# Transfers and weight steps of a fused attention and expert kernel, put at other places of its order

## The chip, the cores and the metric

The kernel runs on one core of a Trainium2 chip. The metric is device time in microseconds, from the start of the program to its end. Three runs of the kernel before took 948.88 to 951.73 us, 950.14 in the median; 0.3% of that is 2.9 us.

## What is computed

Two stages, the second on the output of the first. Attention has 4 batches, 8 heads, 576 positions and 64 values a head; the scores get a causal mask and a bias from a running sum of `s`:

```
scores = q @ k.T / sqrt(64) + minimum(-(cum[i] - cum[j]), 0), causal, cum = cumsum(max(s, 0))
x = (softmax(scores) @ v), heads side by side: 2304 tokens x 512
p = domain_probs / sum(domain_probs)
out = sum over 4 experts e of p[:, e] * (relu(x @ w1[e]) @ w2[e])      # w1: 512 x 1024, w2: 1024 x 512
```

All is float32. The kernel splits each matmul operand into a high part and a rest and adds three products.

## The kernel before

**Three phases.** In the first, attention is planned by a small scheduler (class `Sched`), and expert 0 is computed on seven groups of token tiles (`GROUPS0`, numbered 0 to 6, two or three tiles of 128 tokens each) as soon as their tokens are there, whole for groups 0 to 4 and with the second half of its hidden columns alone for groups 5 and 6. Group results that are ready during attention go to DRAM (`o_d`, "spilled": groups 0 to 2), since their place in SBUF is not free yet. The second phase is what is left of this list (`prog`): the second layer of group 3 and all of groups 4, 5 and 6. The third phase takes the other expert halves (`HALVES`, seven pairs of an expert and half its hidden columns). In it 768 tokens at a time (`PAIRS`, three of them, called g = 0, 1, 2) pass through a first and a second layer, each with seven block products instead of eight, as in Strassen's scheme. The work list has 6 x 3 items and a last one alone (`LONE`: the first half of expert 0, only for g = 2). The order is first layer of item 0, first layer of item 1, second layer of item 0, first layer of item 2, and so on, so that the second layer of the last item stands alone at the end.

**Products.** Each product (`product`) is 12 matmuls on 384 columns. The first layer multiplies in the order 1, 6, 5, 7, 2, 4, 3, the second layer in the order 1, 6, 2, 5, 7, 3, 4. In the second layer the bank of product 1 is copied by ACT (`pass_on`) before product 6 goes on adding to it. Behind each product, `after(o)` runs steps that a table names: operands of the next second layer ("1" to "7": ACT writes the high part, DVE or POOL the rest; "s3" and the like: a sum by DVE that an operand needs) and one step from the list `side`, which holds the splits of the next expert's weights (`w_steps`: sums of weight blocks, then per block ACT the high part and DVE or POOL the rest). `ALL` is the table for the second layer of the last item but one. The last second layer had no steps.

**Sums of operands.** Products 5, 7, 6 and 3 of the first layer read sums of token blocks. `sums_of(g)` makes them in the second phase: it fetches four blocks of g (for g = 1 and 2 from `xf_d` into one of 6 temporary buffers; for g = 0 both parts from `x_d` into operand buffers, which POOL then joins), and POOL makes four sums, each of an add and a split in two instructions. Each sum is stored to `xs_d` (768 KB). For g = 0 the sums also stay in SBUF (`held`), as first operands of the third phase. Operand buffers are a ring of 7 (768 KB each).

**What sets the order.** Each engine works through its instructions in the order in which they were written, and all transfers are issued by one queue, SP. In the second phase the steps (fetches, sums, stores, weight loads and weight splits) carry a position in microseconds of planned PE time, `spent`, which each matmul raises by its planned duration (0.1735 for 384 columns, 0.12 for 256). A step is written when `spent` reaches its position; steps beyond the end follow at the end. So a position says where an instruction stands in every queue and not when it runs. Between the steps stand the loads that belong to `prog` itself: a group's input (`load_x`, into the one buffer `xg`) right behind the last first-layer product of the group before, and the gates of a token block (`prob0`, into one of two buffers `osb`) at the first eviction that needs them. The evictions of the second phase (DVE, `evict0`) multiply a bank by the gates into `acc`. Behind all that stood the 20 loads that bring the spilled results back into `acc`, and then the gates of the first item of the third phase.

The lines that rows name: L1077 fetches blocks for the sums, L1094 stores a sum, L1050 and L1057 fetch operands, L930 a group's input, L1031 gates, L1123 and L1128 weights, L1267 returns spilled results; L1061 adds and subtracts, L448 makes a rest, L461 and L463 a high part; L946 is the rest of a hidden half, L1203 the eviction of the second phase, L1282 the matmuls of the third, L1290 `pass_on`, L1293 the gating, L1405 the updates of `acc`.

Positions before: the sums of g = 1 from 10, those of g = 2 from 28, those of g = 0 from 47; in each, the fetches come first, then the sums 4.7 apart, and each sum's store stands where the next sum begins:

```
yield now, lambda o=o, d=d, a_=a_, b_=b_, op=op: split(o, d, a_, b_, op)
now += 4.7
yield now, lambda o=o: store(o)
```

Of the kernel before, what the change touches and what calls it, by code (L numbers as in the profile page):

```python
# [36 lines left out]
T_PREP = (10.0, 28.0, 47.0)  # L37
T_LOAD = 6.0
T_W1 = 44.0
T_W2 = 53.0  # L40
# [3 lines left out]
ALL = {4: "4", 1: "1", 2: "2", 6: "6", 5: "5", 7: "7", 3: "s3 3"}  # L44
# [286 lines left out]
def body(ctx, tc, qk, qkv0, vp, s, dp, w1, w1s, w2, w2s, out):  # L331
# [731 lines left out]
    def sums_of(g, held):  # L1063
# [7 lines left out]
        def load(part):  # L1071
            if held is not None and not held:
                held.update({o: x_tile() for o in PRODUCTS})
# [21 lines left out]

        for at, part in zip((-8.0, -4.0, 0.0, 4.0) if held is not None else (0.0, 2.0, T_LOAD, T_LOAD + 2.0), order):
            yield at, lambda part=part: load((part,))
        now = 8.0
# [4 lines left out]
        for o, d, a_, b_, op in ((5, (1, 1), (1, 0), (1, 1), ALU.add), (7, (1, 0), (0, 0), (1, 0), ALU.subtract),  # L1103
                                 (6, (0, 0), (1, 1), (0, 0), ALU.subtract), (3, (0, 1), (0, 1), (0, 0), ALU.subtract)):
            yield now, lambda o=o, d=d, a_=a_, b_=b_, op=op: split(o, d, a_, b_, op)
            now += 4.7
            yield now, lambda o=o: store(o)
# [23 lines left out]
    def w_steps(which, begin=False, lone=False):  # L1131
# [24 lines left out]
        def split(o, e):  # L1156
# [8 lines left out]
            if o == (6 if neg else 2) and not begin:  # L1165
# [4 lines left out]
                 ((1, "DVE"), (2, "POOL"), (5, "DVE"), (6, "DVE"), (7, "POOL"), (3, "DVE"), (4, "POOL")) if lone else  # L1170
# [21 lines left out]

    def prob0(b_):
# [6 lines left out]
    def evict0(gi, dt, t):  # L1200
        n0, n1 = GROUPS0[gi][0] * P, GROUPS0[gi][-1] * P + P
        for b_, u0, u1 in blocks_of(n0, n1):
# [5 lines left out]
    steps = sorted(((T_PREP[n] + t, n, k, f) for n, g in enumerate((1, 2, 0)) for k, (t, f) in enumerate(sums_of(g, None if g else held))),  # L1208
                   key=lambda x: x[:3])
    steps.append((T_PREP[1] + 1.0, 9, 0, lambda: (stage_w1(*HALVES[0]), stage_w2(*HALVES[0]))))  # L1210
# [6 lines left out]
    steps.append((T_W1 - 4.0, 9, 0, lambda: w_begin(1, w1_first)))  # L1217
# [7 lines left out]
    for i, x in enumerate(prog):  # L1225
# [16 lines left out]
        else:  # L1242
# [4 lines left out]
            else:  # L1247
                if x[3].done is None:
                    nc.sync.dma_start(out=o_d[dt * P:(dt + 1) * P, n0:n1], in_=tok["osb", x[1]][:, 0:n1 - n0])
                spilled.append((dt, n0, n1))  # L1250
# [14 lines left out]
    for dt, n0, n1 in spilled:  # L1265
        for b_, u0, u1 in blocks_of(n0, n1):
            nc.sync.dma_start(out=acc[dt][b_][:, u0 - TG * b_:u1 - TG * b_], in_=o_d[dt * P:(dt + 1) * P, u0:u1])  # L1267
# [184 lines left out]
    for w_i, (n, g) in enumerate(work):  # L1452
# [20 lines left out]
        if g == 2 and more:  # L1473
            w2_next = w_steps(2, lone=n + 1 == LONE)
            k = 8 if n + 1 == LONE else 4
            side.extend(w2_next[:k])
            del w2_next[:k]
        second_layer(w_i, n, g, plan(steps, EARLY if w_i + 2 < len(work) else ALL if w_i + 2 == len(work) else {}))
# [34 lines left out]
```

## Time and profile before

| | |
|---|---|
| median of three runs | 950.14 us |
| profiled execution | 948.41 us, span 946.6 us |
| PE busy | 915.2 us (97%) |
| DVE, ACT, POOL busy | 706.9, 491.7, 518.2 us |
| transfers | 201.34 MB, mean 213 GB/s |

The profile is of one execution; its times start with the span. PE is TensorE's matmuls, DVE VectorE, ACT ScalarE, POOL GpSimd, SP the queue that issues transfers (SPq in rows). A busy PE is not PE at its peak. A row of a timeline merges like instructions that follow each other, and says in brackets how long the engine was idle before them and what ended that. The granted clock is 1.00 when TensorE runs at full speed and falls towards 0.5 when the throttle halves it.

### The profile page before, as it was taken

What the parts mean: (1) busy time and instruction counts of PE and PEld (TensorE: products, weight loads), DVE (VectorE), ACT (ScalarE), POOL (GpSimd) and SP (SyncE); (2) the same over time, 40 slices, a digit from 0 to 9 for tenths busy, and PEclk for the clock granted to TensorE, in tenths of its full rate; (3) what the DMA queues carried; (4) which work ended last, traced back from release to release, by engine and by line L of the source; (5) the groups of instructions that cost most, each with busy time, mean ns of one, the idle gap of its engine ahead of it and who ended that gap; (6) DMA issues with size and microseconds to landing.
All of it is one profiled execution on the core that took longest, in us unless ns stands there. A gap on an engine that the chain in (4) does not pass through costs nothing.

```text
span 946.6 us, 16511 instructions
## 1 busy us (share of the span) xinstructions
PE 915.2 (97%) x5566; PEld 885.1 (94%) x5566; DVE 706.9 (75%) x1599; ACT 491.7 (52%) x1117; POOL 518.2 (55%) x540
## 2 busy tenths in 40 slices
PE   9999999999999977799999999999999999999996
PEld 6889999999999967699999999999999999999996
DVE  7878887887842536487787878778877887787885
ACT  6898999998841202234443344353344533443542
POOL 4688787887726487016541644362456317443562
PEclk9999999999999997899999999999999999999999
DMA  6788888778426984897666587656875667864201
GB/s 170 189 251 246 224 230 225 224 226 244 133 95 193 337 285 151 283 376 256 220 205 220 196 294 241 202 174 225 292 250 172 214 220 234 287 214 156 84 1 66
DMA packets 132239, 201.34 MB, mean 213 GB/s; under 512 B 11496, under 2 KB 107820, under 8 KB 132156
## 3 DMA queue, kind: packets, MB, share of 16 engines
q1 hardware_dynamic: 132156, 200.30, 66.2%
q8 instruction: 44, 0.72, 0.3%
q14 instruction: 39, 0.32, 0.1%
HBM read 157.34 MB, written 29.05 MB: 197 GB/s over the span
## 4 chain that ended last, share of the span: by engine, by line
PE 54%; DVE 2%; DMA 2%; SPq 1%; ACT 1%; POOL 1%; issue 0%; ACTq 0%; DVEq 0%; POOLq 0%
PE pb L1282 46%; PE mo L1282 8%; DMA osb<-p_d 1%; DVE t L1293 1%; SPq L1267 1%; DMA acc<-o_d 1%; DVE acc L1405 0%; DVE hT_r L448 0%; DVE t L1322 0%; ACT hT_r L461 0%; DVE w1l L448 0%; POOL w1l L448 0%; ACT w1h L461 0%; POOL hT_r L448 0%; ACT pb L1290 0%
## 5 line engine op out<-in xcount | busy, mean ns | idle before, releaser
L1282 PE MATMUL pb<-x,w1h 128*128 128x384 f32 x1064 | 272.1, 336 | 7.0 <-DMA x<-x_d 7.0
L1282 PEld LDWEIGHTS pb<-x,w1h 128*128 128x128 f32 x1064 | 192.5, 189 | 9.2 <-ACT t L1315 8.8
L1282 PE MATMUL pb<-x,w1l 128*128 128x384 f32 x532 | 178.4, 335 | 0.0
L1290 ACT ACTIVATE pb<-pb 128x384 f32<-128x384 f32 x112 | 53.0, 474 | 204.2 <-DVE t L1322 112.1
L448 POOL TENSOR_TENSOR hT_r<-t,hT_r 128x768 fp32r<-128x768 f32 x18 | 33.8, 1876 | 176.3 <-PE pb L1282 147.8
L1282 PE MATMUL pb<-hT_r,w2h 128*128 128x384 f32 x432 | 109.6, 334 | 0.0
L1282 PEld LDWEIGHTS pb<-x,w1l 128*128 128x128 f32 x532 | 100.3, 189 | 0.0
L461 ACT ACTIVATE hT_r<-t 128x768 fp32r<-128x768 f32 x76 | 64.0, 843 | 55.6 <-PE pb L1282 44.3
L762 ACT ACTIVATE a<-a,mx 128x576 f32<-128x576 f32 (+4 forms) x136 | 81.0, 597 | 12.6 <-DVE mx L754 9.3
L1405 DVE TENSOR_TENSOR acc<-pb,acc 128x384 f32<-128x384 f32 x152 | 78.7, 549 | 11.8 <-ACT pb L1290 7.2
L940 PE MATMUL mo<-xg,w1h 128*128 128x384 f32 (+1 forms) x304 | 79.9, 332 | 3.1 <-DMA xg<-x_d 3.1
L1282 PEld LDWEIGHTS pb<-hT_r,w2h 128*128 128x128 f32 x432 | 78.0, 188 | 0.0
L448 DVE TENSOR_TENSOR hT_r<-t,hT_r 128x768 fp32r<-128x768 f32 x58 | 58.4, 1006 | 24.4 <-ACT hT_r L461 23.8
L456 POOL TENSOR_SCALAR a<-a,sm 128x576 f32<-128x576 f32 (+5 forms) x111 | 61.0, 556 | 28.4 <-DVE sm L770 14.4
L1282 PE MATMUL pb<-xg,w2h 128*128 128x384 f32 x288 | 73.3, 335 | 0.7 <-ACT pb L1290 0.7
L1282 PE MATMUL pb<-hT_r,w2l 128*128 128x384 f32 x216 | 72.2, 334 | 0.0
L1322 DVE TENSOR_TENSOR t<-pb,t 128x384 f32<-128x384 f32 x78 | 39.8, 552 | 40.4 <-ACT t L1315 27.5
L1061 DVE TENSOR_TENSOR t<-t 128x768 f32<-128x768 f32 (+1 forms) x42 | 64.6, 1544 | 0.1
L448 POOL TENSOR_TENSOR xg<-t,xg 128x768 fp32r<-128x768 f32 x19 | 43.0, 2261 | 31.8 <-PE pb L1282 31.8
L940 PEld LDWEIGHTS mo<-xg,w1h 128*128 128x128 f32 x304 | 52.7, 193 | 5.6 <-DMA xg<-x_d 4.2
L818 DVE TENSOR_TENSOR aTl<-T,aTh 128x256 fp32r<-128x256 f32 (+2 forms) x103 | 51.2, 508 | 4.9 <-ACT aTh L461 3.6
L1293 DVE SCALAR_TENSOR_TENSOR t<-t,osb 128x768 f32<-128x768 f32 x40 | 47.0, 1177 | 10.3 <-DMA osb<-p_d 9.0
(245 smaller groups left out, 2346.1 us busy)
## 6 DMA issues: line engine op xcount, KB each, us to landing
x<-xs_d SPq DMA_DIRECT2D x68, 768.0 KB
x<-x_d SPq DMA_DIRECT2D x55, 768.0 KB
xs_d<-x SPq DMA_DIRECT2D x12, 768.0 KB
osb<-p_d SPq DMA_DIRECT2D x19, 384.0 KB
w1r<-in_w1s_dram SPq DMA_DIRECT2D x7, 1024.0 KB
w2r<-in_w2s_dram SPq DMA_DIRECT2D x7, 1024.0 KB
KK<-AB_r SPq DMA_DIRECT2D x24, 288.0 KB
xg<-x_d SPq DMA_DIRECT2D x16, 384.0 KB
```

Of the source, the lines that this page charges most:

```text
L448: (nc.gpsimd if e == "POOL" else nc.vector).tensor_tensor(out=out, in0=in0, in1=in1, op=ALU.subtract)
L456: (nc.gpsimd if e == "POOL" else nc.vector).tensor_scalar(out, in_, scale, 1.0 if bias is None else bias, op0=ALU.mult, op1=ALU.mult if bi ...
L461: nc.scalar.activation(out, in_, AF.Copy)
L762: nc.scalar.activation(z[0:n, 0:bb], z[0:n, 0:bb], AF.Exp, bias=tok["mx", c][0:n, k:k + 1], scale=-1.0, accum_out=tok["sm", c][0:n])
L818: nc.vector.tensor_tensor(out=dst, in0=src, in1=h_.bitcast(F32), op=ALU.subtract)
L940: nc.tensor.matmul(t[:, 0:w], wl[q][:, dc, o:o + P], xgt[:, l, dc, 0:w], start=(u == 0), stop=(u == 3 * KD - 1))
L1061: (nc.gpsimd if e == "POOL" else nc.vector).tensor_tensor(out=out, in0=in0, in1=in1, op=op)
L1282: nc.tensor.matmul(ts[u], wv[wl][:, k, 128 * u:128 * u + 128], x[xl_][:, k, :], start=start and k == 0 and n == 0, stop=k == 1 and n == 2, ...
L1290: nc.scalar.activation(out[u], in_[u], AF.Copy)
L1293: (nc.gpsimd if e == "POOL" else nc.vector).scalar_tensor_tensor(out=out, in0=in0, scalar=0.0, in1=in1, op0=ALU.max, op1=op)
L1322: nc.vector.tensor_tensor(out=tmp[name][:, u], in0=ts[u], in1=tmp[name][:, u], op=ALU.add)
L1405: nc.vector.tensor_tensor(out=d, in0=ts[u], in1=d, op=ALU.add)
```

## The change

Seven things move. (1) The positions of the sums stand in a table of their own, `SUM_AT`: fetches, the first sum, the first store. For g = 1 the fetches stand at 0.3 to 1.2, the sums from 2.0 and the stores from 13.5; for g = 2 at 6, 6.5, 16 and 18, from 23 and from 32; for g = 0 at 31 to 36, from 42 (four joins, then sums from 49.6) and from 57. Sums and stores follow each other 4.7 apart. (2) The seven operand buffers that stay in SBUF are asked for in another order. (3) The first weight halves are fetched at 20 and 25, one by one, instead of both at 29. (4) The first layer's weight sums begin at 36 instead of 40 and its splits at 42 instead of 44; the second layer's sums at 50 instead of 53. (5) The 20 return loads (`back`) stand at 48.0 instead of at the end. (6) In the last second layer, operand 3 is made behind product 1 and operand 4 behind product 6; before, both were made in the second layer before it. (7) The weight blocks of the last second layer are split in the order 5, 2, 6, 1, 7, 3, 4, with the sums and the first four inside the second layer before it and the other three inside the last one.

```diff
--- before.py
+++ after.py
@@ -34,14 +34,16 @@
 HALVES = [(e, s) for e in range(1, E) for s in range(2)] + [(0, 0)]
 LONE = len(HALVES) - 1
 LG = 2
-T_PREP = (10.0, 28.0, 47.0)
-T_LOAD = 6.0
-T_W1 = 44.0
-T_W2 = 53.0
+SUM_AT = {1: ((0.3, 0.6, 0.9, 1.2), 2.0, 13.5), 2: ((6.0, 6.5, 16.0, 18.0), 23.0, 32.0), 0: ((31.0, 31.5, 32.0, 36.0), 42.0, 57.0)}
+T_RAW = (20.0, 25.0)
+T_W1 = 42.0
+T_W2 = 50.0
+T_BACK = 48.0
 START = {7: "4"}
 EARLY = {1: "1", 6: "s5", 5: "s7", 7: "2", 3: "s6", 4: "4"}
 REST = {1: "6 5", 6: "s3 7", 5: "3"}
-ALL = {4: "4", 1: "1", 2: "2", 6: "6", 5: "5", 7: "7", 3: "s3 3"}
+ALL = {1: "1", 2: "2", 6: "6", 5: "5", 7: "7"}
+END = {1: "s3 3", 6: "4"}
 LAST = {4: "s5 s7", 3: "s6"}
 FIRST = {1: "s5 s7 1", 6: "s6 6", 5: "2 s3", 4: "5", 3: "7 3"}
 PRODUCTS = (1, 6, 5, 7, 2, 4, 3)
@@ -1070,7 +1072,7 @@
 
         def load(part):
             if held is not None and not held:
-                held.update({o: x_tile() for o in PRODUCTS})
+                held.update({o: x_tile() for o in (3, 4, 1, 2, 5, 7, 6)})
             for i, j in part:
                 if held is None:
                     raw[i, j] = temp()
@@ -1093,9 +1095,9 @@
         def store(o):
             nc.sync.dma_start(out=xsv[g, SUMS[o]], in_=flat4(blocks[o]))
 
-        for at, part in zip((-8.0, -4.0, 0.0, 4.0) if held is not None else (0.0, 2.0, T_LOAD, T_LOAD + 2.0), order):
+        loads, now, out_at = SUM_AT[g]
+        for at, part in zip(loads, order):
             yield at, lambda part=part: load((part,))
-        now = 8.0
         if held is not None:
             for i, j in order:
                 yield now, lambda i=i, j=j: join(i, j)
@@ -1103,8 +1105,9 @@
         for o, d, a_, b_, op in ((5, (1, 1), (1, 0), (1, 1), ALU.add), (7, (1, 0), (0, 0), (1, 0), ALU.subtract),
                                  (6, (0, 0), (1, 1), (0, 0), ALU.subtract), (3, (0, 1), (0, 1), (0, 0), ALU.subtract)):
             yield now, lambda o=o, d=d, a_=a_, b_=b_, op=op: split(o, d, a_, b_, op)
+            yield max(now, out_at), lambda o=o: store(o)
             now += 4.7
-            yield now, lambda o=o: store(o)
+            out_at += 4.7
 
     stage = {}
 
@@ -1167,7 +1170,7 @@
 
         order = (tuple((o, "DVE") for o in ((1, 2, 4, 3, 6, 5, 7) if which == 1 else (1, 2, 3, 4, 6, 5, 7))) if begin else
                  ((5, "POOL"), (1, "POOL"), (2, "POOL"), (6, "POOL"), (4, "POOL"), (7, "DVE"), (3, "DVE")) if which == 1 else
-                 ((1, "DVE"), (2, "POOL"), (5, "DVE"), (6, "DVE"), (7, "POOL"), (3, "DVE"), (4, "POOL")) if lone else
+                 ((5, "DVE"), (2, "POOL"), (6, "DVE"), (1, "DVE"), (7, "POOL"), (3, "DVE"), (4, "POOL")) if lone else
                  ((1, "DVE"), (2, "DVE"), (5, "DVE"), (6, "DVE"), (7, "POOL"), (3, "DVE"), (4, "DVE")))
         return [sums] + [lambda o=o, e=e: split(o, e) for o, e in order]
 
@@ -1190,6 +1193,12 @@
     spilled = []
     pbuf = {}
 
+    def back():
+        for dt, n0, n1 in spilled:
+            for b_, u0, u1 in blocks_of(n0, n1):
+                nc.sync.dma_start(out=acc[dt][b_][:, u0 - TG * b_:u1 - TG * b_], in_=o_d[dt * P:(dt + 1) * P, u0:u1])
+        spilled.append(None)
+
     def prob0(b_):
 
         if pbuf.get(b_ % 2) != b_:
@@ -1205,16 +1214,15 @@
 
     last_l1 = max(i for i, x in enumerate(prog) if x[0] == "l1e")
     held = {}
-    steps = sorted(((T_PREP[n] + t, n, k, f) for n, g in enumerate((1, 2, 0)) for k, (t, f) in enumerate(sums_of(g, None if g else held))),
-                   key=lambda x: x[:3])
-    steps.append((T_PREP[1] + 1.0, 9, 0, lambda: (stage_w1(*HALVES[0]), stage_w2(*HALVES[0]))))
+    steps = [(t, g, k, f) for g in (1, 2, 0) for k, (t, f) in enumerate(sums_of(g, None if g else held))]
+    steps += [(T_RAW[0], 9, 0, lambda: stage_w1(*HALVES[0])), (T_RAW[1], 9, 0, lambda: stage_w2(*HALVES[0])), (T_BACK, 9, 0, lambda: back())]
     w1_first, w2_first = [], []
 
     def w_begin(which, steps):
         steps.extend(w_steps(which, True))
         steps.pop(0)()
 
-    steps.append((T_W1 - 4.0, 9, 0, lambda: w_begin(1, w1_first)))
+    steps.append((T_W1 - 6.0, 9, 0, lambda: w_begin(1, w1_first)))
     for n in range(4):
         steps.append((T_W1 + 2.0 * n, 9, n, lambda: w1_first.pop(0)()))
         steps.append((T_W2 + 1.5 + 2.0 * n, 9, n, lambda: w2_first.pop(0)()))
@@ -1247,6 +1255,7 @@
             else:
                 if x[3].done is None:
                     nc.sync.dma_start(out=o_d[dt * P:(dt + 1) * P, n0:n1], in_=tok["osb", x[1]][:, 0:n1 - n0])
+                assert None not in spilled
                 spilled.append((dt, n0, n1))
         if x[0] in ("l1", "l2"):
             while steps and steps[0][0] <= spent:
@@ -1262,9 +1271,6 @@
         f()
     while wsteps:
         wsteps.pop(0)()
-    for dt, n0, n1 in spilled:
-        for b_, u0, u1 in blocks_of(n0, n1):
-            nc.sync.dma_start(out=acc[dt][b_][:, u0 - TG * b_:u1 - TG * b_], in_=o_d[dt * P:(dt + 1) * P, u0:u1])
     bA, bB, bC, bM = ([t[:, 0:TG] for t in ts] for ts in (pb[0:2], pb[2:4], pb[4:6], mo))
     def h_part(o, l):
         if o == 3:
@@ -1472,10 +1478,12 @@
             side.extend(w1_next)
         if g == 2 and more:
             w2_next = w_steps(2, lone=n + 1 == LONE)
-            k = 8 if n + 1 == LONE else 4
+            k = 5 if n + 1 == LONE else 4
             side.extend(w2_next[:k])
             del w2_next[:k]
-        second_layer(w_i, n, g, plan(steps, EARLY if w_i + 2 < len(work) else ALL if w_i + 2 == len(work) else {}))
+        if n == LONE:
+            side.extend(w2_next)
+        second_layer(w_i, n, g, plan(steps, EARLY if w_i + 2 < len(work) else ALL if w_i + 2 == len(work) else END))
         while side:
             side.pop(0)()
```

## Rows read from the trace of the kernel before

**Rows 1.** Stretches: length, busy (count) of PE, PEld, DVE, ACT, POOL, clock, DMA share, GB/s.

```profile
338.40:341.20 2.80, 0.00 (x0) 0.00 (x0) 0.00 (x0) 0.00 (x0) 2.63 (x3) 1.00 1.07 389
341.20:371.70 30.50, 22.72 (x96) 19.73 (x97) 20.82 (x22) 3.82 (x8) 27.88 (x16) 0.78 0.53 190
371.70:386.40 14.70, 14.70 (x86) 14.42 (x84) 3.57 (x6) 4.40 (x9) 2.03 (x2) 1.00 0.62 186
386.40:393.40 7.00, 0.05 (x2) 0.04 (x1) 2.20 (x3) 1.60 (x3) 0.00 (x0) 0.75 0.91 291
393.40:409.70 16.30, 16.30 (x85) 16.30 (x86) 14.63 (x23) 7.22 (x12) 4.11 (x2) 0.90 1.06 378
...
923.90:928.90 5.00, 0.28 (x3) 0.02 (x1) 3.69 (x6) 3.58 (x7) 3.15 (x3) 1.00 0.00 0
```

**Rows 2.** Waits of PE over the span: total, times, longest (us).

```profile
PE pb L1282 <- DMA x<-x_d: 7.0, 1, 7.0
PE pb L1282 <- ACT pb L1290: 5.4, 2, 4.7
```

**Rows 3.** Timeline of SP, 290 to 425: start, length, line, transfer, count.

```profile
307.42 1.90 SPq L930 DMA_DIRECT2D xg<-x_d  x4
...
312.55 4.75 SPq L1077 DMA_DIRECT2D t<-xf_d  x2
...
334.44 2.98 SPq L930 DMA_DIRECT2D xg<-x_d  x4
...
342.66 0.36 SPq L1094 DMA_DIRECT2D xs_d<-x  x1
...
357.83 16.37 SPq L1094 DMA_DIRECT2D xs_d<-x  x4
374.25 11.43 SPq L1267 DMA_DIRECT2D acc<-o_d  x20
...
386.25 0.39 SPq L1050 DMA_DIRECT2D x<-x_d  x1
```

**Rows 4.** Timeline of POOL, same stretch; in brackets idle time before, releaser.

```profile
291.63 1.85 POOL L1061 TENSOR_TENSOR t<-t 128x768 f32<-128x768 f32 x1 [11.84 <-DMA t<-xf_d]
...
308.46 1.84 POOL L448 TENSOR_TENSOR x<-t,x 128x768 fp32r<-128x768 f32 x1
322.34 1.84 POOL L1061 TENSOR_TENSOR t<-t 128x768 f32<-128x768 f32 x1 [12.03 <-DMA t<-xf_d]
...
327.63 2.30 POOL L1061 TENSOR_TENSOR t<-t 128x768 f32<-128x768 f32 x1
...
333.37 1.84 POOL L1061 TENSOR_TENSOR t<-t 128x768 f32<-128x768 f32 x1
```

**Rows 5.** Timeline of DVE, same stretch.

```profile
348.07 1.02 DVE L1203 TENSOR_TENSOR acc<-pb,osb 128x384 f32<-128x384 f32 x2 [16.37 <-DMA osb<-p_d]
349.01 0.68 DVE L1061 TENSOR_TENSOR hx_f<-w2r 128x512 f32<-128x512 f32 x1
...
350.33 2.33 DVE L1061 TENSOR_TENSOR hx_f<-hx_f,w2r 128x512 f32<-128x512 f32 x1
...
360.48 0.55 DVE L946 SCALAR_TENSOR_TENSOR hT_r<-mo,hT_r 128x384 fp32r<-128x384 f32 x1
```

**Rows 6.** Chain that ended last, 374 to 392: start, length, what.

```profile
382.41 0.43 SPq L1267
...
385.78 4.35 DMA osb<-p_d
```

**Rows 7.** The same chain, 920 to 947.

```profile
924.17 1.04 DVE t L1061
...
928.45 0.38 ACT pb L1290
...
928.88 5.99 PE pb L1282 x24
934.87 2.08 PE mo L1282 x12
```

## The prediction, made before the change was run

> **What bounds the kernel now.** I read the page first. PE is busy 97% of the span, and in the 40 slices its digit is below 9 in slices 15 to 17 and in the last one only. Everywhere else PE is full, so only time that PE loses in those places can be won. Then I asked for the windows around them [rows 1]. The stretch 371.7 to 386.4 is the first product pass without a hole: 84 matmuls (seven products of 12; the count catches two neighbours) in 14.7 us, 0.175 us each. Measured with that, 96 matmuls of token group 6 should take 16.8 us and take 30.5 (13.7 lost); ahead of them PE stands for 2.8 us, behind them the next pass waits 7.0 us and then runs 16.3 us for 84 matmuls (1.6 lost, granted clock 0.90); near the end 5.0 us are idle. The waits of PE name who ended the two longest [rows 2]: an operand fetch (7.0) and ACT's copy of a bank (4.7 of 5.4 in two). The reader is to see in the transfer queue [rows 3] why: SP issues in order, so a store of a sum that waits for POOL holds up every fetch behind it. It is parked until 342.66 for the last sum of the second group and until 357.83 for the first of the third; four stores take it to 374.2, then 20 loads that bring spilled results back take 11.43 us, and only at 386.25 is the operand fetch issued for which PE waits.
>
> **The end (operands 3 and 4, last weight blocks).** The chain [rows 7] shows DVE adding for operand 3 at 924.17, then ACT working through operands and weight blocks until it reaches the bank copies; the second of them starts at 928.45, PE goes on at 928.88, and its first 24 matmuls take 5.99 us where 12 later take 2.08 (so 4.16 for 24: 1.83 lost to the lower clock after the hole). The change puts operand 3 behind product 1, operand 4 behind product 6, and blocks 7, 3, 4 behind products 1, 6, 2 of the last second layer, that is all behind these copies. Nothing is added: the same ACT, DVE and POOL instructions. Are they late now? Product 1 of the last layer ends at 923.9 [rows 1]. After it DVE adds (1.04), ACT and POOL split operand 3 (about 2.7 us), POOL splits block 7 (about 1.9): 929.5, and PE, unhindered, reaches product 7 at 924 + 3 x 2.08 = 930.2. Operand 3 and block 3 are wanted at 932.3, operand 4 and block 4 at 934.4; each has 2 us or more. The new order of the earlier blocks (5, 2, 6, 1) leaves block 1's low part to DVE at about 922.0, while PE wants it at about 922.3: at worst 0.5 us. So 4.9 idle and 1.83 of clock go, 0.3 comes back: 6.4 us.
>
> **The queue in the middle.** Steps carry positions in planned PE time, and the order in which SP issued before fixes where they fall: the input load of group 5 lies at 28.4, that of group 6 at 48.0 to 48.6. I follow SP through the new order. POOL's first sums start when SP's first fetches land; those move only from behind to ahead of two small loads (1 us), so POOL starts about 2 us earlier than 291.63 and ends its first group, which took 18.7 us, at 308.2 instead of 310.3 [rows 4]. The last two fetches of the second group were issued at 312.55 to 317.3 [rows 3], and POOL stood 12.03 us for fetches until 322.34 [rows 4]. Now two go right behind the first four, and two wait for temporary buffers that POOL frees by about 301. So POOL runs on from 308.2. What that group costs: 20.3 us before (322.34 to 342.66, when its last store leaves), against 18.7 for the first; its first two sums, beside which DVE works too, took 5.29 and 5.74 where a sum of the first group takes 18.7 / 4 = 4.67 [rows 4]. Weight sums move 4 positions earlier, into this group; with three sums at 5.6 it takes 21.5 us and ends at 329.7, against 342.66.
>
> The Trainium skill bears on that price: "SBUF — State Buffer", section "Who interferes with whom", says a DVE instruction with two SBUF inputs and a GpSimd instruction that reads SBUF exclude each other for the whole instruction. The trace agrees in kind: a DVE sum takes 0.68 us alone and 2.33 behind a POOL one, a POOL sum 1.85 and 2.30 [rows 4, 5]. By the rule taken fully, eight DVE instructions of 0.68 would add 5.5 us to POOL's group where I add 2.8; the forecast would be 2.7 us later.
>
> Does the input of group 5 come too late? Its load (4 issues, 1.90 us, issued at 307.42) now stands behind the last store of the first group, so it leaves at 308.6 to 310.3. In front of it in the transfers are stores and weight loads that keep the queue full; transfers of 768 KB follow each other there at about 2.1 us (an estimate from 0.37 MB per us, the 378 GB/s of a full stretch in [rows 1]). It lands at about 316 to 319; PE wants it at 319.8. Hidden by 1 to 3 us.
>
> SP then meets fetches of the third group (landing long before POOL wants them), the four stores of the second group, the last at 329.8, and behind that, at position 48.0, the 20 return loads: 8.6 us at an issue time of 0.43 each [rows 6], 11.43 as before [rows 3]; I take the latter, since the transfers ahead of them are full until 335. That is the price of the change: right behind them stands the load of group 6's input, issued at 334.44 before and now at 341.2. A load of the same size took 4.35 us from issue to use right behind the return loads [rows 6], some 1 to 1.5 of it for the last of these; so 3 to 4.35, and as here SP's pace leaves less ahead I take 3: PE starts group 6 at 344.1 instead of 341.2, after 5.7 us of standing instead of 2.8. That costs 2.9 us, and the lower clock comes as before.
>
> What is late next in group 6? The gate load behind the input lands at 348, as before (348.07 [rows 5]). But DVE then had 5.9 us of second-layer weight sums in front of its evictions and hidden halves (349.01 on, the hidden halves beginning at 360.48). Those sums now stand ahead of that wait (position 50 instead of 53) and are done by 338. DVE reaches the hidden halves at about 356, 4.6 us earlier; PE, in its second layer from 354, waits 2 us there and has 10 us of matmuls left, so group 6 ends at about 366 instead of 371.7: 5.7 won.
>
> The next pass: POOL had its third group in 342.7 to about 374, when the last of the four stores leaves [rows 3], so 31 us; from 329.7 it ends at about 361, before PE needs the sums of it. Nothing is left between SP and the fetches of the next pass: they go out one product after another from about 368, each 12 us before use. So the 7.0 us wait and 1.6 of clock go, and the smaller of the two waits for a bank copy (5.4 - 4.7 = 0.7 [rows 2]). Sum of the middle: 5.7 + 7.0 + 1.6 + 0.7 = 15.0.
>
> **Sum.** 15.0 + 6.4 = 21.4. The profiled execution took 948.41 (span 946.6 and 1.8 around it): 927.0. The median of the runs shown is 950.14, 1.7 above it: 950.1 - 21.4 = 928.7, said as 929.
>
> **Bounds of what the trace doesn't show.** The return loads beside full transfers: 8.6 to about 15 us, that is 2.8 better or 3.6 worse. The temporary buffers for the two waiting fetches: freed at about 301, or only with the last sum at 308; then group 5's input lands at 323 to 325 and PE loses 3 to 5 us. The buffers for the last two sums of the second group, freed when earlier stores land: 0 to 3 us. The clock in group 6: 0.78 granted before [rows 1]; between full (3 better) and one more stretch of half clock (3 worse).
>
> **Rivals.** *The return loads are nearly free* (0.17): they issue in 8.6 us and the clock stays up in group 6. For it: SP's shortest issues; against it: 1.75 MB more ahead of the input. The middle gives 19 to 21, the time is 923.
>
> *They cost what they save* (0.18): buffers are freed late, group 5's input is late by 4 and group 6's start by 4 to 6 more; the middle gives only the 7.0, 1.6 and 0.7 of the next pass and loses some 2 of them. For it: stores still wait for POOL, since POOL sets when a sum exists wherever its store stands, so the queue is not freed as the few words promise. With the end, 950.1 - 6.4 - 7 = 937.
>
> *Slower* (0.07): one mechanism, the last store of the second group. Seven operand buffers serve both the sums and the fetched blocks of the third group, and fetches of these now stand ahead of three stores; if a sum has to wait for a buffer whose store is behind such a fetch, POOL and SP hold each other up, and the return loads, group 6's input and its gate all follow. Group 6 ends 36 us after that store by the walk above (329.8 to 366), and gains at the end and in the next pass are worth 15.7, so the change turns slower when the store leaves after 351; it was at 342.66 before. At 356 the time would be 955.
>
> The likeliest case has 0.58, its own range 924 to 934.
>
> **How the numbers follow.** 0.58 at 929, 0.17 at 923, 0.18 at 937, 0.07 beyond 943. The range 919 to 940 leaves out the slower case, the worst of the third and the best of the second. About 0.3% (2.9 us) is what a measurement of this kernel can tell from no change; faster by more than that has 0.91, within it 0.03 (a weak form of the last rival), slower 0.06.
>
> **What would show it.** In the profile after: POOL without the 12 us hole before its second group; return loads starting near 330 and the load of group 6's input behind them near 341; a PE wait for that input longer than 2.8 us; no 7.0 us wait for an operand fetch; DVE's weight sums ahead of its wait for the gate; at the end PE going from product 1 to 6 without the 4.7 us wait. The prediction is wrong if the input of group 5 is waited for by more than 3 us, if the return loads keep SP much longer than 11 us, or if group 6 ends after 371.

## The result and the profile after

The changed kernel takes 933.52 us in the median of four runs (933.35 to 934.08), the kernel before, on the same chip, 949.94: a ratio of 0.9826 with a 95% interval of 0.9809 to 0.9843. It is faster by 16.4 us; 21.4 were predicted (929, range 919 to 940). The profiled execution after took 933.43 us, with a span of 931.7, 14.9 below the one before. The line numbers of this kernel: L932 loads a group's input, L1033 gates, L1052 an operand; L1096 stores a sum, L1199 returns spilled results, L1212 is the eviction of the second phase, L1063 adds, L942 and L957 are a group's first and second layer, L948 is the rest of a hidden half, L1288 the matmuls of the third phase, L1296 `pass_on`, L1299 the gating, L1321 ACT's copy of a bank in front of it, L1411 the updates of `acc`; L450 makes a rest, L465 a high part. In the kernels of the experiments they stand up to two off.

The stretches that answer to [rows 1], with the same columns:

```profile
338.60:349.20 10.60, 0.00 (x0) 0.00 (x0) 0.00 (x0) 0.00 (x0) 10.34 (x8) 0.60 0.77 227
349.20:371.90 22.70, 21.65 (x98) 19.81 (x99) 13.79 (x18) 3.52 (x7) 12.37 (x8) 0.81 0.57 194
371.90:386.40 14.50, 14.50 (x85) 14.50 (x84) 7.08 (x11) 6.12 (x12) 0.00 (x0) 1.00 0.81 267
386.40:401.10 14.70, 14.70 (x87) 14.70 (x86) 13.65 (x20) 7.16 (x12) 3.96 (x2) 1.00 1.03 365
```

The reader is to see three things. PE now stands for 10.6 us ahead of group 6, where it stood for 2.8. Group 6 then takes 22.7 us instead of 30.5, so that it ends at 371.9, where it ended at 371.7. And the next pass follows without a gap at full clock, where 7.0 us of standing and 1.6 us of clock lay. The next pass begins at 371.71 (before: 371.72), so the 14.9 us by which the spans differ are all won behind group 6: these 8.6, and 6.3 more, nearly all at the end. The waits of PE, as in [rows 2], say the same:

```profile
PE mo L942 <- DMA xg<-x_d: 11.5, 2, 10.7
PE pb L1288 <- ACT pb L1296: 1.0, 1, 1.0
```

The timeline of SP, answering to [rows 3], shows why:

```profile
314.51 4.57 SPq L1052 DMA_DIRECT2D x<-x_d  x3
319.17 1.53 SPq L1096 DMA_DIRECT2D xs_d<-x  x1
320.75 2.66 SPq L1052 DMA_DIRECT2D x<-x_d  x1
323.50 11.42 SPq L1096 DMA_DIRECT2D xs_d<-x  x3
334.97 10.40 SPq L1199 DMA_DIRECT2D acc<-o_d  x20
345.47 1.91 SPq L932 DMA_DIRECT2D xg<-x_d  x4
347.48 0.42 SPq L1033 DMA_DIRECT2D osb<-p_d  x1
...
373.98 0.36 SPq L1052 DMA_DIRECT2D x<-x_d  x1
```

The operand fetch leaves at 373.98 instead of 386.25. The input of group 6 leaves at 345.47 instead of 334.44, because the last store in front of it waits for POOL until 334.5 and 20 return loads follow. Behind it stands a gate load, at 347.48. POOL and DVE, answering to [rows 4, 5]; POOL's lines come first:

```profile
289.85 1.84 POOL L1063 TENSOR_TENSOR t<-t 128x768 f32<-128x768 f32 x1 [10.15 <-DMA t<-xf_d]
...
308.48 1.86 POOL L1063 TENSOR_TENSOR t<-t 128x768 f32<-128x768 f32 x1
...
318.44 2.29 POOL L1063 TENSOR_TENSOR t<-t 128x768 f32<-128x768 f32 x1
...
330.98 1.32 POOL L465 TENSOR_SCALAR x<-t 128x768 fp32r<-128x768 f32 x1 [5.29 <-DMA xs_d<-x]
...
334.50 8.05 POOL L1063 TENSOR_TENSOR t<-x 128x768 f32<-128x768 f32 x4
```

```profile
335.12 2.21 DVE L1063 TENSOR_TENSOR hx_f<-w2r,hx_f 128x512 f32<-128x512 f32 x1
354.01 0.56 DVE L1212 TENSOR_TENSOR acc<-pb,osb 128x384 f32<-128x384 f32 x1 [16.68 <-DMA osb<-p_d]
...
362.48 1.01 DVE L948 SCALAR_TENSOR_TENSOR hT_r<-mo,hT_r 128x384 fp32r<-128x384 f32 x2
...
366.14 0.54 DVE L1212 TENSOR_TENSOR acc<-pb,osb 128x384 f32<-128x384 f32 x1
```

POOL's second group of sums begins right behind the first, the 12 us hole is gone, but the last sum waits 5.29 us for a store of an earlier one to land. DVE has its weight sums done at 337.3 and then waits for the gate until 354.0.

Whose gate is it? A gate is loaded at the first eviction that needs it, and the evictions that begin at 354.01 are the four of group 5's second layer; group 6's own four begin at 366.14, and their gate is loaded later (356.75). So the gate load behind group 6's input, which the expectations below call group 6's, is group 5's. It holds up group 6 in two ways: group 5's results keep their banks until it is there, and in DVE's queue its evictions stand in front of group 6's hidden halves.

PE's first layer of group 6 ends at 362.4, just when DVE reaches the hidden halves, and PE goes on without a wait (timeline of PE):

```profile
362.36 2.55 PE L957 MATMUL pb<-hT_r,w2h 128*128 128x384 f32 x8
```

The end, in the chain of waits [rows 7], has no hole any more; 48 matmuls take 8.32 us, so 24 take 4.16:

```profile
911.57 8.32 PE pb L1288 x48
...
928.25 0.56 DVE acc L1411
```

### The profile page after: what moved, and what is told of

Same layout as the page of the kernel before. It is cut to its first block, busy times and chain, and to the rows that moved or that the text cites. A ratio compares the mean times of both kernels' runs of the same rounds, so it can differ in the third digit from the quotient of the medians.

```text
span 931.7 us, 16516 instructions
## 1 busy us (share of the span) xinstructions
PE 911.6 (98%) x5566; PEld 882.4 (95%) x5566; DVE 704.3 (76%) x1599; ACT 491.9 (53%) x1117; POOL 516.4 (55%) x540
## 4 chain that ended last, share of the span: by engine, by line
PE 88%; DVE 4%; ACT 2%; DMA 2%; SPq 2%; issue 1%; POOL 1%; ACTq 0%; POOLq 0%; DVEq 0%
PE pb L1288 49%; PE mo L1288 8%; PE mo L942 7%; PE mo L957 5%; PE pv L841 5%; PE T L791 3%; PE S L745 3%; PE S L742 2%; PE pb L957 1%; PE pb L942 1%; PE X L791 1%; DMA xs_d<-x 1%; SPq L1199 1%; ACT a L764 1%; DMA xg<-x_d 1%
## 5 line engine op out<-in xcount | busy, mean ns | idle before, releaser
L1288 PE MATMUL pb<-x,w1h 128*128 128x384 f32 x1064 | 270.7, 335 | 0.0
L1288 PEld LDWEIGHTS pb<-x,w1h 128*128 128x128 f32 x1064 | 191.4, 188 | 2.0 <-ACT t L1321 1.6
L1288 PE MATMUL pb<-x,w1l 128*128 128x384 f32 x532 | 177.8, 334 | 0.0
L1296 ACT ACTIVATE pb<-pb 128x384 f32<-128x384 f32 x112 | 53.1, 475 | 202.5 <-DVE t L1328 112.1
L450 POOL TENSOR_TENSOR hT_r<-t,hT_r 128x768 fp32r<-128x768 f32 x18 | 34.8, 1935 | 176.6 <-PE pb L1288 128.7
L1288 PE MATMUL pb<-hT_r,w2h 128*128 128x384 f32 x432 | 109.6, 334 | 0.0
L1288 PEld LDWEIGHTS pb<-x,w1l 128*128 128x128 f32 x532 | 99.8, 188 | 0.0
L942 PE MATMUL mo<-xg,w1h 128*128 128x384 f32 (+1 forms) x304 | 81.4, 338 | 11.5 <-DMA xg<-x_d 11.5
L764 ACT ACTIVATE a<-a,mx 128x576 f32<-128x576 f32 (+4 forms) x136 | 81.0, 598 | 13.1 <-DVE mx L756 10.2
L1411 DVE TENSOR_TENSOR acc<-pb,acc 128x384 f32<-128x384 f32 x152 | 78.8, 550 | 10.1 <-ACT pb L1296 6.5
L1288 PEld LDWEIGHTS pb<-hT_r,w2h 128*128 128x128 f32 x432 | 78.0, 188 | 0.0
L450 DVE TENSOR_TENSOR hT_r<-t,hT_r 128x768 fp32r<-128x768 f32 x58 | 58.8, 1013 | 23.0 <-ACT hT_r L463 22.5
L1288 PE MATMUL pb<-xg,w2h 128*128 128x384 f32 x288 | 73.3, 335 | 1.0 <-ACT pb L1296 1.0
L1288 PE MATMUL pb<-hT_r,w2l 128*128 128x384 f32 x216 | 72.2, 334 | 0.0
L942 PEld LDWEIGHTS mo<-xg,w1h 128*128 128x128 f32 x304 | 53.9, 197 | 14.1 <-DMA xg<-x_d 12.8
L1063 DVE TENSOR_TENSOR t<-t 128x768 f32<-128x768 f32 (+1 forms) x42 | 63.4, 1517 | 0.1
L450 POOL TENSOR_TENSOR xg<-t,xg 128x768 fp32r<-128x768 f32 x19 | 42.9, 2259 | 35.1 <-ACT xg L463 35.1
L756 DVE CUSTOM_DVE_ANT_0 a<-S,mask 128x448 f32<-128x448 f32 (+4 forms) x107 | 48.1, 456 | 7.4 <-PE S L742 5.8
```

What stands on the lines that cost most here:

```text
L450: (nc.gpsimd if e == "POOL" else nc.vector).tensor_tensor(out=out, in0=in0, in1=in1, op=ALU.subtract)
L756: nc.vector.tensor_tensor_reduce(out=z[0:n, j0:j1], in0=tok["S", (c, pi)][0:n, 0:j1 - j0], in1=mask[0:n, 448 - a + j0:448 - a + j1], scale ...
L764: nc.scalar.activation(z[0:n, 0:bb], z[0:n, 0:bb], AF.Exp, bias=tok["mx", c][0:n, k:k + 1], scale=-1.0, accum_out=tok["sm", c][0:n])
L942: nc.tensor.matmul(t[:, 0:w], wl[q][:, dc, o:o + P], xgt[:, l, dc, 0:w], start=(u == 0), stop=(u == 3 * KD - 1))
L1063: (nc.gpsimd if e == "POOL" else nc.vector).tensor_tensor(out=out, in0=in0, in1=in1, op=op)
L1288: nc.tensor.matmul(ts[u], wv[wl][:, k, 128 * u:128 * u + 128], x[xl_][:, k, :], start=start and k == 0 and n == 0, stop=k == 1 and n == 2, ...
```

## The experiments

The theory: the change is three gains (the end, the operand fetch, group 6), and the third was lost because the return loads stand in front of group 6's input and gate. The buffer rival: the last store, held by POOL's wait for a buffer, was to blame. The clock rival: the low clock after the long standing was. Letters in an expectation are that expectation's own.

**The end alone.** The kernel before, with parts 6 and 7 of the change:

```diff
-ALL = {4: "4", 1: "1", 2: "2", 6: "6", 5: "5", 7: "7", 3: "s3 3"}
+ALL = {1: "1", 2: "2", 6: "6", 5: "5", 7: "7"}
+END = {1: "s3 3", 6: "4"}
...
-                 ((1, "DVE"), (2, "POOL"), (5, "DVE"), (6, "DVE"), (7, "POOL"), (3, "DVE"), (4, "POOL")) if lone else
+                 ((5, "DVE"), (2, "POOL"), (6, "DVE"), (1, "DVE"), (7, "POOL"), (3, "DVE"), (4, "POOL")) if lone else
...
-            k = 8 if n + 1 == LONE else 4
+            k = 5 if n + 1 == LONE else 4
...
```

> The kernel before with the change at its end alone (operands 3 and 4, the last weight blocks and their order), nothing moved in the middle. Theory: the end is a term of its own, worth the hole of 4.9 us and 1.8 us at the lower clock, less a little: 6.4 us, so 943.5 us against 949.9, and the middle of the trace as before (PE waits 7.0 us for an operand fetch). Rival: the order of the weight blocks only moves the wait from the bank copy to a weight block; then 2 us or less are won, 948 or more.

942.67 us; ratio 0.992 (0.9907 to 0.9934), that is 7.5 us. From the same product on, which starts at 890.73 before and at 889.73 here, to the ends of the spans (946.6 and 939.1) the traces differ by 6.5 us; the other 1.0 lies ahead of it, where the edit changes nothing. The step held.

**The buffer wait.** The kernel after; the fourth fetch of the third group stands behind the second group's last store, so no sum waits for its buffer:

```diff
-SUM_AT = {... 0: ((31.0, 31.5, 32.0, 36.0), 42.0, 57.0)}
+SUM_AT = {... 0: ((31.0, 31.5, 32.0, 46.2), 42.0, 57.0)}
```

> The changed kernel with the fourth fetch of the third group (the block that took the last free operand buffer) put behind the last store of the second group, at position 46.2 instead of 36. Theory: POOL's wait of 5.3 us in the last sum of the second group is a wait for an operand buffer whose store had not landed; with the buffer free the last store leaves at about 329.4 instead of 334.6, the return loads, the input of group 6 and its gate all follow 5 us earlier, and group 6 ends about 5 us earlier: 929 us against 933.5. Rival: the buffer that is freed is another, or POOL waits for the late block instead: POOL's hole only moves and the time stays at 933 to 934.

932.0 us; ratio 0.9805 (0.9791 to 0.9819). That is 1.5 us below the change, and the two intervals overlap; in the trace group 6 ends 1.0 us earlier. POOL's 5.29 us wait is gone (instead it waits 3.50 us at 339.7 for the late block) and the last store leaves at 329.5, as predicted for the change. But the loads then take longer, and the input leaves when it left in the change (timeline of SP, and SP's own waits between 300 and 390):

```profile
331.75 0.36 SPq L1052 DMA_DIRECT2D x<-x_d  x1
332.16 13.45 SPq L1199 DMA_DIRECT2D acc<-o_d  x20
345.70 0.38 SPq L932 DMA_DIRECT2D xg<-x_d  x1
```

```profile
SPq L1199 <- DMA xs_d<-x: 2.5, 2, 1.5
...
SPq L1199 <- DMA x<-x_d: 1.7, 1, 1.7
```

In three places the loads waited for earlier transfers to land, 4.2 us in all, 1.7 of it for the very fetch that the edit puts right in front of them; and this fetch had itself waited 1.8 us. The 929 expected were not reached: with the buffer wait gone, the loads still stand in front of the input, and longer. As the edit gives back in front of the loads most of what it takes from POOL's wait, it doesn't show what the buffer wait costs by itself.

**The return loads behind the input, and behind the gate.** The kernel after; two positions that differ by one small load in SP's order:

```diff
-T_BACK = 48.0
+T_BACK = 49.0        # first kernel: behind group 6's input
+T_BACK = 51.0        # second kernel: behind the gate load too
```

> The changed kernel with the 20 return loads at position 49 instead of 48, that is behind the load of group 6's input and still ahead of the gate load. Theory A (the return loads stand in front of both, and the gate is the second lock): the input lands by about 340 and the 10.7 us wait falls to 2 or 3, but the gate still comes at about 350, PE stops after two of four first-layer products, and group 6 ends only about 4 us earlier: 929.5 us. Theory B (the input alone holds PE): group 6 ends 8 to 9 us earlier, 924.5 us. Theory C (the place of the return loads does not matter, the transfers behind them are limited by bytes): 933.5.

934.66 us; ratio 0.9838 (0.9822 to 0.9855): nothing won against the change, so 924.5 is out, and by the number 933.5 came nearest. The mechanism is theory A's all the same: PE begins group 6 at 340.6, but then a bank waits for an eviction of group 5, and that for the gate, at 354.5 instead of 354.0 in the change. The granted clock falls in that wait, and the second layer, from 363.43 to the next pass at 373.60, takes 10.2 us at 0.83, against 8.6 us at 1.00 in gate_and_late_fetch below. These are the timelines of SP, PE and DVE:

```profile
338.42 12.46 SPq L1199 DMA_DIRECT2D acc<-o_d  x20
350.98 0.38 SPq L1033 DMA_DIRECT2D osb<-p_d  x1
```

```profile
355.13 1.01 PE L942 MATMUL pb<-xg,w1h 128*128 128x384 f32 x2 [8.34 <-DVE acc L1212]
```

```profile
354.52 0.56 DVE L1212 TENSOR_TENSOR acc<-pb,osb 128x384 f32<-128x384 f32 x1 [16.87 <-DMA osb<-p_d]
```

> The changed kernel with the return loads at position 51, behind the input and the gate load of group 6; only their place in the transfer queue differs. Theory A: the input lands by about 340 and the gate by about 344, hidden halves begin at about 352 instead of 362, no long stretch of low clock; group 6 ends near 361 instead of 371.9: 923.5 us. Theory B: the same as with the loads behind the input alone, 924.5. Theory C: 933.5.

922.95 us; ratio 0.9713 (0.97 to 0.9726), 10.6 us better than the change, with only SP's order different. The gate leaves ahead of the loads, DVE's wait ends 9.3 us earlier, and group 6 ends at 361.4 (timelines of SP and DVE, then the stretches of group 6 and of the pass behind it):

```profile
338.68 0.48 SPq L1033 DMA_DIRECT2D osb<-p_d  x1
339.21 12.60 SPq L1199 DMA_DIRECT2D acc<-o_d  x20
```

```profile
344.70 0.56 DVE L1212 TENSOR_TENSOR acc<-pb,osb 128x384 f32<-128x384 f32 x1 [6.84 <-DMA osb<-p_d]
```

```profile
340.80:361.40 20.60, 20.07 (x98) 17.77 (x99) 14.91 (x15) 3.52 (x7) 20.00 (x12) 0.92 0.73 244
361.40:376.10 14.70, 14.70 (x86) 14.70 (x85) 8.49 (x14) 6.12 (x12) 2.68 (x2) 1.00 0.86 266
```

So input and gate are two locks in a row. The first of the two edits won nothing because the second lock was still shut. The gate alone in front of the loads was not run, so what the late input costs by itself is not shown.

**The same loads, moved in the kernel before, or not moved in the kernel after.** `back` as in the change, called in the kernel before behind both gate loads (group 5's and group 6's); and the kernel after with the loads at the end:

```diff
+T_BACK = 67.0        # kernel before
...
-T_BACK = 48.0        # kernel after
+T_BACK = 1000.0
```

> The kernel before with one edit: the 20 return loads stand behind the second gate load of group 6 (position 67) instead of at the end, so SP issues them from about 343.9 us, in the 14 us in which it stood parked for the first store of the third group, and they are done before 357.8. Theory (the queue order alone is the middle's gain): the four stores still leave until 374.2, the operand fetch follows there instead of at 386.25 and lands before 386.4, so the 7.0 us wait, 1.6 us of clock and 0.7 us of a bank copy go: 950.0 - 9.3 = 940.7 (940 to 942). Rival 1 (the middle's gain needs the sums to be made earlier): the fetch goes out no earlier than 382, since the stores take longer behind the return loads; 946 to 950. Rival 2 (a half gain): the first pass runs through, but the third group's joins wait behind 1.75 MB of traffic and the sums come later; 943 to 946.

939.6 us; ratio 0.9884 (0.9868 to 0.9899), 10.9 us, where the theory said 9.3. The loads go into 14 us in which SP stood for POOL's next sum, and the operand fetch leaves at 375.29; the pass behind group 6 runs through, though the stores and sums are where they were:

```profile
344.95 14.41 SPq L1197 DMA_DIRECT2D acc<-o_d  x20
359.46 15.20 SPq L1095 DMA_DIRECT2D xs_d<-x  x4
374.75 0.46 SPq L1032 DMA_DIRECT2D osb<-p_d  x1
375.29 0.96 SPq L1051 DMA_DIRECT2D x<-x_d  x1
```

> The kernel after with the 20 return loads put back at the end of the queue, behind the stores of the third group; all else of the change stays. Theory (they are in the way wherever something urgent stands behind them): group 6 gets its input at 335.5 and its gate at 338.7 and ends at about 361.4, as with the loads behind the gate; but now the loads run from about 364.6 to 376 and the operand fetch of the next pass goes out at about 376.8 instead of 366.5; where it took 7.15 us from issue to PE's start in the kernel before, PE stands from 376.1 to 380 to 384: 923 + 4 to 8 + 1.6 for the clock = 928 to 933, said as 931. Rival (only group 6's two loads matter, and the operand fetch has slack): 923.

932.89 us; ratio 0.9816 (0.9802 to 0.9831): as fast as the change. Group 6 ends at 361.4, as with the loads behind the gate, and the 10 us are given back one pass later: third-phase gate and operand fetch stand behind the loads, and PE waits (PE's waits, then SP):

```profile
PE pb L1288 <- ACT t L1321: 8.0, 1, 8.0
```

```profile
364.57 11.45 SPq L1199 DMA_DIRECT2D acc<-o_d  x20
376.11 0.38 SPq L1033 DMA_DIRECT2D osb<-p_d  x1
```

**Both mends together.** Loads behind the gate, and the late fourth fetch:

> The return loads behind the gate (position 51) and the fourth fetch of the third group behind the last store of the second (46.2): the two edits that were tried singly. Theory: singly the late fetch won 1.5 us, because the return loads were the next lock; with these out of the way, the last store leaves at 329.5, the input at 332.3, and PE's 2.0 us wait for group 6's input goes with the 1.7 us that 3.4 us of half clock cost behind it: 923.0 - 3.7 = 919.3 (918 to 921). Rival 1 (the sums of the third group become the lock): POOL waits 3.5 us for the late fetch, the third group ends later, and the operand fetch behind its last store makes the next pass wait: 923 to 926. Rival 2 (no difference): input and gate queue behind the fetch's transfer, 922 to 923.

923.55 us; ratio 0.972 (0.9704 to 0.9736): no difference from the loads behind the gate alone, rival 2 of its expectation. PE's waits for group 6's input fall to 0.7 us and the clock stays up, and group 6 still ends at 361.5, since the gate is there at 344.15 and not earlier, and PE now waits 2.3 us for hidden halves (stretch, DVE, PE's waits):

```profile
340.50:361.50 21.00, 19.00 (x98) 16.71 (x98) 14.07 (x15) 3.52 (x7) 20.32 (x13) 1.00 0.68 221
```

```profile
344.15 0.56 DVE L1212 TENSOR_TENSOR acc<-pb,osb 128x384 f32<-128x384 f32 x1 [5.61 <-DMA osb<-p_d]
```

```profile
PE pb L957 <- DVE hT_r L948: 2.3, 2, 1.2
```

So the clock rival doesn't hold for these two kernels: granted clocks of 0.92 and 1.00 in group 6 end at the same time. DVE behind the gate sets the end. From DVE's first hidden half to the end of group 6 it is 9.4 us with the loads behind the gate (351.99 to 361.4) and 9.3 here (352.20 to 361.5), and it is 9.4 in the change (362.48 to 371.9).

**DVE's weight sums behind the gate again.** The kernel with the loads behind the gate; `T_W2` also places the four splits of these weights, so they move with the sums:

```diff
-T_W2 = 50.0
+T_W2 = 53.0
```

> The kernel with the return loads behind the gate (922.95), with one edit: the second layer's weight sums stand at 53 again instead of 50, so that on DVE two of group 6's evictions, which wait for the gate, come ahead of the four sums. It tests the step of the prediction that put 5.9 us of weight sums between the gate and the hidden halves. Theory (DVE behind the gate sets group 6's end): the gate lands at 344.7 as before; with four sums (some 6 us beside POOL) behind it, the hidden halves begin 4 to 6 us later and group 6 ends as much later: 927 to 929, said as 928. Rival (something else sets the end of group 6, the sums are hidden): 923.

932.03 us; ratio 0.9804 (0.9785 to 0.9823). The theory held in kind, and the cost was 9.1 us, not 5 (932.03 lies outside the 927 to 929 expected). The four sums alone take DVE from 345.0 to 352.4, beside POOL, and the hidden halves begin at 357.99 instead of 351.99 and the first two come one by one between splits (timeline of DVE):

```profile
344.06 1.02 DVE L1212 TENSOR_TENSOR acc<-pb,osb 128x384 f32<-128x384 f32 x2 [12.50 <-DMA osb<-p_d]
345.00 1.70 DVE L1063 TENSOR_TENSOR hx_f<-w2r 128x512 f32<-128x512 f32 x1
346.74 2.22 DVE L1063 TENSOR_TENSOR w2r<-w2r 128x512 f32<-128x512 f32 x1
348.88 1.31 DVE L1063 TENSOR_TENSOR hx_f<-hx_f,w2r 128x512 f32<-128x512 f32 x1
350.22 2.18 DVE L1063 TENSOR_TENSOR hx_f<-w2r,hx_f 128x512 f32<-128x512 f32 x1
```

**What the small edits do in the kernel before.** Loads behind the gate (here behind both gates) and the end (two); these and `T_W2 = 50.0` (three); `T_W2 = 50.0` alone:

> The kernel before with two edits alone: the return loads behind the second gate load of group 6 (position 67, as in back_alone), and the end of the change (operands 3 and 4 and the last three weight blocks inside the last second layer, as in tail_only). Sums, stores, fetches and weight loads stay where they were. Theory (the two gains add): 950.2 - 10.9 - 7.5 = 931.8 (930.5 to 933), so the two edits give what the whole change gave (933.5), and the moved sums and stores earn nothing until the return loads stand behind the gate. Rival (the gains overlap, or the sums' places do part of it): 935 to 938.

932.38 us; ratio 0.9805 (0.9786 to 0.9825): the gains add, and three of the seven parts (6 and 7, and 5 in a better place) give what all seven gave.

> The kernel with two edits (return loads behind the gate, the end of the change; 932.4) and a third: the second layer's weight sums at 50 instead of 53. Sums, stores, fetches and weight loads stay where they were before. Theory (of the moved sums and stores only what brings the gate earlier earns anything; the rest of group 6's gain is the place of DVE's weight sums): the gate lands at 347.9 as with the two edits, DVE has its sums behind it and needs 7.3 us of evictions and splits to the hidden halves (as in the kernel with the loads behind the gate, 344.7 to 352.0), so they begin at 355.2 instead of 358.8 to 361.5 and group 6 ends at 364.6 instead of 371.7: 925.4 (924 to 927). Rival (stores and fetches in their new places are what frees group 6): 931 to 932.5.

931.39 us; ratio 0.981 (0.9792 to 0.9828): the rival, and no clear gain on the two edits. Group 6 ends at 366.0, 5.7 us earlier than in the kernel before (the theory said 364.6), but the gain isn't kept. POOL's third group and the stores behind it are as late as before (until 374.5), and the passes behind group 6 wait: 0.5 us for POOL's sums, and 1.6 us for ACT and DVE, which the chain of waits follows back to a gate load issued at 374.64, right behind those stores. These two waits are about half of what is lost again; the rest was not followed up. These are PE's waits and that piece of the chain:

```profile
PE pb L1289 <- ACT t L1322: 1.6, 1, 1.6
...
PE pb L1289 <- POOL x L450: 0.5, 1, 0.5
```

```profile
374.64 5.77 DMA osb<-p_d
...
380.50 0.97 DVE t L1300
```

So with group 6 earlier, the stores behind POOL's late sums are the next to be waited for. In the kernel with the loads behind the gate, which also has parts 1 to 4, the last store leaves at 364.2; which of these parts brings that was not told apart.

> The kernel before with one edit: the second layer's weight sums at 50 instead of 53. Theory (two locks in a row): group 6 ends some 6 us earlier, but stores and return loads still hold the next operand fetch at 386.25, so PE waits for it 13 us instead of 7: 950 (949 to 951), with the clock perhaps 1 us worse. Rival (group 6 sets the rest, the operand fetch moves along): 943 to 945.

948.79 us; ratio 0.9988 (0.9979 to 0.9998). The theory held: the 5 us won in group 6 come back in the next wait, now 12.2 us long where it was 7.0.

Loads and the rest set against each other, medians in us, all with the end in its new form:

| | loads at the end | at 48, ahead of the input | behind the gate |
|---|---|---|---|
| sums, stores, fetches, weights as before | 942.7 | not run | 932.4 |
| as in the change | 932.9 | 933.5 | 923.0 |

Read across, the loads behind the gate instead of at the end are worth 10.3 and 9.9 us; read down, the other parts are worth 9.8 and 9.4. So the two nearly add, and the earlier sums, stores, fetches and weights earn their 10 us even with the loads at the end. At 48 the loads' place earns nothing (933.5 against 932.9).

## Why the prediction was right in its range and 5 us off

**The end**: 6.4 predicted, 6.5 in the traces. **The operand fetch and its clock**: 7.0 + 1.6 predicted, and they are gone. The prediction gave two causes at once, POOL's third group done by about 361 (the last store left at 362.0) and the loads out of the way. The runs show that the second is the one that counts: moving the return loads alone removes this wait (back_alone), and moving everything else leaves one of 8.0 us (back_at_end). The 0.7 us of a bank copy was not won; 1.0 us of such a wait stands in the trace after.

**Group 6**: 5.7 predicted, none won; this is the step that failed, and by the prediction's own sign ("if group 6 ends after 371") it was wrong here. Of the "5.7 us of standing instead of 2.8" there were 10.67. Step by step:

| | predicted | measured |
|---|---|---|
| POOL's first group ends | 308.2 | 308.48 |
| second group, its end | 21.5 us, 329.7 | 20.7 us and a wait of 5.29, 334.5 |
| PE's waits for group 5's input | none | 0.7 us in all |
| last store of the second group | 329.8 | 334.56 |
| 20 return loads | 11.4 us | 10.40 us |
| group 6's input issued, PE starts | 341.2, 344.1 | 345.47, 349.25 |
| gate lands, hidden halves begin | 348, 356 | 354.0, 362.48 |
| group 6 ends | 366 | 371.87 |

One number was outside what was allowed for: the wait for an operand buffer, bounded at 0 to 3 us and taken at nothing, was 5.29. It made the last store 4.8 us late. The walk behind it held within 1.6 us a step: the loads took 1.0 less than said, and from the gate's issue to its use it was 6.5 us where the walk, with the gate right behind the input at about 343, leaves 5. From the gate to the hidden halves it was 8.5 (8 said), from there to the end 9.4 (10 said). One link of it came out otherwise: PE was to wait 2 us for DVE, and it did not, since it worked at a granted clock of 0.50 to 0.55 from 349.2 to 358.4 and reached its second layer only when DVE did. What the time would have been without the buffer wait is not shown: in fetch4_late the store leaves at 329.5, the return loads take 13.45 us, 2.0 more than assumed and inside the bounds, and the input leaves at 345.70, but a fetch moved in front of the loads does part of that.

The prediction saw the loads ahead of the input, named them the price of the change and put it at 2.9 us, by which PE was to start later than in the kernel before. Against the loads behind the gate the price is 933.52 less 922.95, 10.6 us. The prediction did not ask how early the gate could land. It took it "at 348, as before" without a working, though its issue moved from 338.53 to behind the loads. That DVE's weight sums stood in the way was right in kind (5.9 us said, 9.1 measured with the gate early and the splits moved too).

For POOL's second group, the rule of the Trainium skill ("SBUF — State Buffer", "Who interferes with whom") that the two engines exclude each other, taken fully, gave an estimate of 5.5 us more than the first; 2.8 were added; it took 2.1 more (20.7 against 18.6). The trace agrees that the two engines slow each other (318.44: 2.29 us instead of 1.85). Whether the exclusion is full it doesn't show, since part of DVE's work fell into POOL's wait of 5.29 us.

Of the rivals, "they cost what they save" came nearest in its sum, with nothing won in group 6; its 937 was 3.5 too slow, since group 6 lost nothing net. "Slower" named the mechanism that worked, a sum of the second group that waits for an operand buffer because of the third group's fetches; fetch4_late bears it out, since with the fourth fetch out of the way the wait is gone (which store was waited for, the trace doesn't tell). Its size was far off: the last store left at 334.6, far from 351. That the total fell into the range is owed to the two terms that held, the end and the next pass.

## What to carry to other kernels

In an in-order transfer queue, ask of every batch that is not urgent what the first urgent thing behind it is, down to the smallest: one small gate load on the wrong side of 20 loads was worth 11.7 us. Where several engines take turns at being late, a step that removes one lateness is worth only the distance to the next: judge such edits together. DVE's weight sums and splits at their earlier place were worth 0.6 us alone, nothing clear beside the loads and the end, and 9.1 with all the other parts in place. All seven parts, with the loads behind the gate, are worth 27. An early place for work that an engine does while it would otherwise wait is only worth something if the time that it frees isn't lost again at the next wait.

## What was not expected of the hardware

The issue time of the same 20 loads differed with what had been issued before them: 10.40 us in the kernel after, 11.13 to 11.45 at the end of the queue, 12.44 to 12.60 behind group 6's input, 13.45 to 15.05 in the five kernels in which an operand fetch had been issued some 5 us or less before. Part of it is seen as waits for such a transfer to land (4.2 us in fetch4_late), although the loads touch none of its data; what ties them together the traces don't show, and it stays open.

The granted clock read 0.60 over the 10.6 us in which PE stood, and 0.81 over group 6 behind it. Inside group 6 it was 0.50 from 349.2 to 353.5 (the level of 1.2 GHz), 0.55 to 358.4 and 1.00 from there. What that cost by itself wasn't told apart, because PE and DVE came to the second layer of group 6 at the same time. Where PE stood in the middle of group 6 (back_behind_input) the low clock behind it did show: its second layer took 10.2 us at 0.83 instead of 8.6 at 1.00.
